# Attention heads as a software pipeline, with more PSUM banks and operands padded to 128 rows

## Chip, cores and metric

One core of a Trainium2 chip. The metric is the device time of one execution in microseconds (us). The kernel before takes 913.33 us (median of 15 runs, 910.32 to 918.20).

## The reference

Local attention with a window of 32 and 8 global tokens, for 8 batches of 8 heads (576 tokens, 64 columns), then a mixer block: token mixing (576 x 576) and a channel MLP (512 to 2048 to 512).

```python
mask = np.abs(pos[:, None] - pos[None, :]) <= 32
mask = mask | is_global[:, None] | is_global[None, :]
scores = np.where(mask, scale * np.matmul(q, k.transpose(0, 1, 3, 2)), -1e9)
attn = softmax(scores)                               # cut: written out in the reference
x = np.matmul(attn, v)                               # then heads side by side: (8, 576, 512)
a1 = alpha1 * x + beta1
u = x + lam * np.einsum('ts,bsd->btd', w_tok, a1)    # token mixing
a2 = alpha2 * u + beta2
out = u + lam * (np.maximum(a2 @ w_ch1, 0.0) @ w_ch2)
```

## The kernel before

One head (cut). Q and K are transposed through one PSUM tile (PSUM is the memory that this kernel's matmuls write their results to; a bank is a part of it). The scores are nine blocks of 128x128 (K=64, so 64 rows of the array) and five narrow matmuls for the global columns. In the value product each of the five query tiles starts with the global keys, a matmul over 8 rows, followed by one or two over 128 rows.

```python
for h in range(H):
    emit_B1(b - 1, h)                  # one piece of the batch before: load X, 1/denominator, XL, token mixing
    ...                                # loads of q, k, v, casts
    for c in range(NT):
        nc.tensor.transpose(out=trps[:, c, :], in_=qn16[:, c, :], identity=identb)
    nc.vector.tensor_copy(out=QT, in_=trps)             # QT, KT: [64, ...]
    for c in range(NT):
        nc.tensor.transpose(out=trps[:, c, :], in_=kn16[:, c, :], identity=identb)   # same bank
    nc.vector.tensor_copy(out=KT, in_=trps)
    ...                                # V's global rows, in the score tile; vg_ext: [8, 65]
    for c in CHUNKS: ...               # scores, K=64 rows
    nc.tensor.matmul(out=pvps[0:8, 512:1024], lhsT=kgT[...], rhs=QTf[:, 0:512], ...) # global scores
    nc.scalar.activation(out=PT, in_=scps[:, 0:SCORE_F], func=AF.Exp, scale=0.125)
    nc.vector.tensor_tensor(out=PT, in0=PT, in1=mask, op=ALU.mult)
    nc.scalar.activation(out=pgc, in_=pvps[0:8, PV_GCB:1024], func=AF.Exp, scale=0.125)  # [8, 640]
    for t in range(NT):
        nc.tensor.matmul(out=pvps[:, ...], lhsT=pgc[:, gsl], rhs=vg_ext, start=True, stop=False)   # 8 rows
        for ci, bi in enumerate(tbis):
            nc.tensor.matmul(out=pvps[:, ...], lhsT=PT[:, ...], rhs=rhs, start=False, ...)         # 128 rows
    ...                                # global rows into the score tile, copies to xstg and xg
# after 8 heads: store xstg to DRAM, scatter-add the global rows; emit_B1 loads it again as X
```

The softmax here doesn't subtract the row's maximum and nothing guards it: scores larger than these inputs give would overflow.

## Time and profile before

| stage | us | what fills it |
|---|---|---|
| setup | 0 to 62 | loads and preparation of weights |
| attention and token mixing | 62 to 640 | TensorE about seven tenths busy, granted clock mostly half |
| channel MLP | 640 to 912 | TensorE full, full clock |

The profile's page cuts the span in 40 slices: a digit is the busy share in tenths, and the row PEclk gives TensorE's granted clock. A timeline line gives start, duration, engine, line of the kernel, operation, output<-inputs, the weights' rows*columns, then the moving operand's rows x columns, and in brackets the idle time before it with what ended it. The prediction shows the lines of before that its reading rests on.

### The profile page before, as it was taken

The page shows a single profiled execution, that of the slowest core. Times are in us where ns is not written, and L with a number is a line of the kernel's source. Part 1 is how long each engine was busy: PE and PEld are TensorE (multiplying, and loading weights), DVE is VectorE, ACT ScalarE, POOL GpSimd, SP SyncE. Part 2 cuts the span into 40 slices and gives each one's busy share as a digit, 9 for nine tenths or more (in the row PEclk, how much of TensorE's full clock was granted, in tenths as well). Part 3 has the DMA queues.
Part 4 walks back from the last instruction along what each step waited for, and adds up shares of the span by engine and source line. Part 5 has one row for each costly group of instructions (what it writes and reads, how often), then busy time and mean ns, then how long its engine had stood idle before and what let it go on. Part 6 is the DMA issues. An engine that isn't in the chain of part 4 may idle for free.

```text
span 912.1 us, 13226 instructions
## 1 busy us (share of the span) xinstructions
PE 720.2 (79%) x5044; PEld 435.1 (48%) x5091; DVE 346.6 (38%) x865; ACT 331.9 (36%) x641; POOL 155.2 (17%) x295
## 2 busy tenths in 40 slices
PE   0158776976976976976976976935999999999998
PEld 0125544544544544544544544513665665665664
DVE  2654335635545635645645645515001001001001
ACT  0014443333333433433443333311552552552551
POOL 0035232232233232233222222100000000000000
PEclk9999999955755855755855755857999999999999
DMA  4825344454454454454454453225222222223101
GB/s 133 346 75 148 89 139 127 142 155 128 134 163 128 136 162 128 140 157 127 138 157 127 142 152 106 96 72 235 111 87 97 88 87 99 88 87 99 60 29 52
DMA packets 119111, 113.24 MB, mean 124 GB/s; under 512 B 90760, under 2 KB 91288, under 8 KB 116488
## 3 DMA queue, kind: packets, MB, share of 16 engines
q1 hardware_dynamic: 110840, 93.01, 32.2%
q0 software_dynamic: 8208, 19.40, 6.8%
q8 instruction: 40, 0.66, 0.3%
q14 instruction: 23, 0.19, 0.1%
HBM read 76.95 MB, written 35.42 MB: 123 GB/s over the span
## 4 chain that ended last, share of the span: by engine, by line
PE 72%; DVE 16%; DMA 6%; ACT 3%; issue 3%; SPq 0%; POOL 0%; POOLq 0%; ACTq 0%; DVEq 0%
PE chps L482 15%; PE hps L473 13%; PE scps L389 8%; PE tkps L293 7%; PE pvps L417 6%; PE pvps L412 4%; PE trps L374 4%; PE trps L371 4%; PE pvps L402 3%; DMA w2raw<-in_moe_w_ch_dram 3%; PE utps L307 3%; DVE XL L283 2%; DVE X L279 2%; DVE QT L372 2%; DVE KT L375 2%
## 5 line engine op out<-in xcount | busy, mean ns | idle before, releaser
L476 ACT ACTIVATE HT<-hps,bias1T 128x288 bf16<-128x288 f32 x256 | 127.7, 501 | 162.2 <-PE hps L473 135.2
L473 PE MATMUL hps<-UT,W 128*128 128x288 bf16 x1024 | 153.0, 285 | 23.2 <-DMA UT<-utdram 20.6
L482 PE MATMUL chps<-W,HT 128*128 128x512 bf16 (+1 forms) x608 | 150.4, 379 | 0.4
L473 PEld LDWEIGHTS <-W 128*128 128x128 bf16 x1024 | 98.5, 97 | 68.7 <-issue 28.9
L486 DVE TENSOR_TENSOR ob<-chps,U 128x512 f32<-128x512 f32 (+1 forms) x40 | 27.6, 690 | 242.7 <-PE chps L482 242.7
L293 PE MATMUL tkps<-XL,wtT 128*128 128x512 bf16 (+3 forms) x185 | 71.1, 492 | 32.4 <-DVE XL L283 29.4
L405 ACT ACTIVATE PT<-scps 128x1192 f16<-128x1192 f32 x64 | 74.5, 1164 | 55.8 <-PE scps L394 53.0
L359 ACT CAST vext<-vn 128x320 f16<-128x320 f32 x64 | 29.3, 458 | 178.4 <-PE scps L426 176.9
L482 PEld LDWEIGHTS <-HT 128*128 128x128 bf16 (+1 forms) x640 | 62.9, 100 | 64.1 <-issue 3.4
L389 PE MATMUL scps<-QT,KT 64*128 64x128 bf16 x576 | 72.2, 270 | 12.7 <-DVE vg_ext L384 12.1
L408 ACT ACTIVATE pgc<-pvps 8x640 f16<-8x640 f32 x64 | 44.4, 693 | 79.5 <-PE pvps L402 79.1
L412 PE MATMUL pvps<-vg_ext,pgc 8*128 8x65 f16 x320 | 71.3, 223 | 0.0
L417 PE MATMUL pvps<-voext,PT 128*128 128x65 f16 x448 | 67.9, 230 | 0.0
L360 POOL MEMSET vext<- 128x5 f16 x64 | 8.0, 125 | 334.8 <-PE scps L426 334.7
L317 POOL DMA_DIRECT2D vn<-in_v_dram x63 | 58.1, 922 | 29.2 <-ACT xg L438 25.0
L435 DVE COPY xstg<-pvps 128x320 f32<-128x320 f32 x64 | 31.3, 490 | 83.1 <-PE pvps L417 83.1
L417 PEld LDWEIGHTS <-PT 128*128 128x128 f16 x576 | 40.1, 108 | 42.8 <-DVE PT L406 22.8
L371 PE MATMUL trps<-identb,qn 128*64 128x128 bf16 x320 | 42.3, 284 | 22.4 <-DVE KT L375 22.4
L394 PE MATMUL scps<-qgT,KT 64*128 64x8 bf16 x320 | 58.5, 201 | 0.0
L372 DVE COPY QT<-trps 64x640 bf16<-64x640 bf16 x64 | 30.9, 482 | 67.1 <-PE scps L394 60.6
L374 PE MATMUL trps<-identb,kn 128*64 128x128 bf16 x320 | 41.5, 286 | 17.2 <-DVE QT L372 16.8
L389 PEld LDWEIGHTS <-KT 64*128 64x128 bf16 x576 | 51.1, 120 | 7.4 <-issue 5.9
(95 smaller groups left out, 839.8 us busy)
## 6 DMA issues: line engine op xcount, KB each, us to landing
xdram<-xstg SPq DMA_DIRECT2D x8, 1300.0 KB, 5.8
X<-xdram SPq DMA_DIRECT2D x8, 1300.0 KB, 6.8
udram<-U SPq DMA_DIRECT2D x8, 1280.0 KB, 5.7
U<-udram SPq DMA_DIRECT2D x8, 1280.0 KB, 5.8
qn<-in_q_dram SPq DMA_DIRECT2D x63, 160.0 KB, 2.9
kn<-in_k_dram SPq DMA_DIRECT2D x63, 160.0 KB, 2.4
vn<-in_v_dram POOLq DMA_DIRECT2D x63, 160.0 KB, 3.4
vo<-in_v_dram POOLq DMA_DIRECT2D x64, 128.0 KB, 3.4
```

What stands on the lines that cost most here:

```text
L293: nc.tensor.matmul(out=tkps[0:tsz, :], lhsT=wtT[0:ssz, sc, t * P : t * P + tsz], rhs=st["XL"][0:ssz, sc, :], start=(sc == 0), stop=(sc == 4),)
L317: eng.dma_start(out=dst, in_=src_flat[bh * S : bh * S + SPAD, :].rearrange("(c p) d -> p c d", p=P))
L371: nc.tensor.transpose(out=trps[:, c, :], in_=qn16[:, c, :], identity=identb)
L374: nc.tensor.transpose(out=trps[:, c, :], in_=kn16[:, c, :], identity=identb)
L389: nc.tensor.matmul(out=scps[:, bi * P : (bi + 1) * P], lhsT=KTf[:, c : c + P], rhs=QT[:, t, :], start=True, stop=True)
L394: nc.tensor.matmul(out=scps[:, GR_OFF + 8 * si : GR_OFF + 8 * si + 8], lhsT=KTf[:, c : c + P], rhs=qgT[:, 8 * h : 8 * h + 8], start=True, ...
L405: nc.scalar.activation(out=PT, in_=scps[:, 0:SCORE_F], func=AF.Exp, bias=0.0, scale=0.125)
L412: nc.tensor.matmul(out=pvps[:, t * PV_T : t * PV_T + PV_T], lhsT=pgc[:, gsl], rhs=vg_ext, start=True, stop=False)
L417: nc.tensor.matmul(out=pvps[:, t * PV_T : t * PV_T + PV_T], lhsT=PT[:, bi * P : (bi + 1) * P], rhs=rhs, start=False, stop=(ci == len(tbis) ...
L473: nc.tensor.matmul(out=hps, lhsT=W1[:, cc, ec * P : (ec + 1) * P], rhs=UT[:, cc, tsl], start=(cc == 0), stop=(cc == 3))
L476: nc.scalar.activation(out=HT[:, ec, tsl], in_=hps, func=AF.Relu, bias=bias1T[:, ec : ec + 1], scale=1.0)
L482: nc.tensor.matmul(out=chps[0:tsz, :], lhsT=HT[:, ec, t * P : t * P + tsz], rhs=W2[:, ec, :], start=(ec == 0), stop=(ec == 15))
```

## The change

Its intent: keep TensorE from waiting for the copies that empty its PSUM tiles, by separate banks and by putting another head's matmuls where it waited; spread the token mixing; and pad the operands of 8 and 64 rows with zeros to 128. The core of the diff, with cuts:

```diff
+        pads = {"pgz": [], "vgz": []}                       # two of each, zeroed once on GpSimd
+            pads["pgz"].append(pPad.tile([P, SPAD], FP16, name=f"pgz{i}"))
+            pads["vgz"].append(pPad.tile([P, PV_T], FP16, name=f"vgz{i}"))
+        for nm, shp in (("QTz", [P, NT, P]), ("KTz", [P, NT, P]), ("qgTz", [P, 64]), ("kgTz", [P, 64])):
 ...
+        def partA(b, h):   # loads, Q transposes (trq), K transposes (free part of scps), scores, exp
-                nc.vector.tensor_copy(out=QT, in_=trps)
+            nc.vector.tensor_copy(out=QT[0:64], in_=trq)      # QT is a padded tile
 ...
+        def partC(st):     # global scores, V's global rows, in a new bank smp
-                pgc = pA.tile([8, SPAD], FP16, name="pgc")
+            pgc = pads["pgz"][(b * 8 + h) % 2]
 ...
+        def partB(st, xstg, xg):   # mask, value product, global rows, copies
 ...
             for h in range(H):
+                st = partA(b, h)
+                if prev is not None:
+                    partB(prev, prev["xstg"], prev["xg"])     # value product of the head before
+                partC(st)
+                emit_B1(b - 1, h)
-                utps = psB_tr.tile([P, 4, P], FP32, name="utps")
+                utps = psB_tok.tile([P, 4, P], FP32, name="utps", tag="tkps")
```

## The prediction

> **What bounds the kernel now.** I read the page first: the slices, then the chain that ended last, then the timeline of one head, then the table by stretches of time.
>
> ```profile
> PE   0158776976976976976976976935999999999998
> PEclk9999999955755855755855755857999999999999
> PE 72%; DVE 16%; DMA 6%; ACT 3%; issue 3%; SPq 0%; POOL 0%; POOLq 0%; ACTq 0%; DVEq 0%
> ```
>
> There are three stages: setup to about 62 us, attention with token mixing from there to about 604 us (seven tenths busy on TensorE, granted clock mostly half), and the channel MLP from 640 us (saturated, full clock). The diff does not touch the first and third, about 62 and 272 us. The second, 542 us for 64 heads, is where anything can be won. The chain is mostly TensorE with a strong VectorE share, so one must see whether TensorE is full or waits. One head on the timeline:
>
> ```profile
> 403.52 0.26 PE L389 MATMUL scps<-QT,KT 64*128 64x128 bf16 x1 [0.30 <-DVE vg_ext L384]
> 405.32 0.69 PE L374 MATMUL trps<-identb,kn 128*64 128x128 bf16 x5 [0.40 <-DVE QT L372]
> 406.58 0.69 PE L371 MATMUL trps<-identb,qn 128*64 128x128 bf16 x5 [0.57 <-DVE KT L375]
> 409.72 0.27 PE L401 MATMUL pvps<-QT,kgT 64*8 64x128 bf16 x1 [0.29 <-DVE xstg L437]
> ...
> 406.45 0.76 DVE L406 TENSOR_TENSOR PT<-PT,mask 128x1192 f16<-128x1192 f16 x1
> 413.84 0.76 DVE L406 TENSOR_TENSOR PT<-PT,mask 128x1192 f16<-128x1192 f16 x1
> ```
>
> The mask multiplication comes once a head, so the period is 413.84 - 406.45 = 7.39 us. In it TensorE stands still four times, 0.30 + 0.40 + 0.57 + 0.29 = 1.56 us, each time for a VectorE copy that empties a single PSUM buffer: the transposes of Q and K share one bank (trps), pvps has one buffer, and the transpose of V's global rows sits in the score tile. So 5.83 us of TensorE are left. Once a batch something larger comes:
>
> ```profile
> PE tkps L293 <- DVE XL L283: 25.2, 6, 4.2
> 359.71 0.58 PE L293 MATMUL tkps<-XL,wtT 128*128 128x512 bf16 x1 [4.20 <-DVE XL L283]
> ```
>
> Token-mixing matmuls stand in TensorE's order ahead of heads that could run, and TensorE waits 4.2 us for two VectorE operations of 2.8 us. The batch period, from the starts of that VectorE operation (147.8 and 559.0, six batches apart), is 68.5 us.
>
> ```profile
> 364.00:366.00 2.00, 2.00 (x13) 0.91 (x11) 0.48 (x1) 1.16 (x1) 0.00 (x0) 0.50 0.00 0
> 370.00:372.00 2.00, 2.00 (x21) 1.29 (x21) 0.79 (x4) 0.82 (x3) 0.28 (x3) 1.00 0.00 0
> 314.00:316.00 2.00, 1.18 (x15) 0.81 (x14) 1.75 (x4) 0.94 (x2) 0.00 (x0) 1.00 1.02 416
> 316.00:318.00 2.00, 1.59 (x17) 0.91 (x17) 0.62 (x3) 0.64 (x3) 0.21 (x2) 0.99 0.96 376
> 318.00:320.00 2.00, 1.70 (x17) 1.26 (x16) 0.83 (x5) 0.92 (x2) 1.61 (x2) 0.50 1.15 291
> ```
>
> The columns after the stretch are its length, busy time of TensorE, weight loads, VectorE, ScalarE and GpSimd, and then the granted clock. The clock becomes full about 10 us after the dense token-mixing work begins (0.50 at 364, 1.00 at 370) and falls back once TensorE is only about 70% busy (314 to 318). That happens in every batch: some 14 to 17 us at full clock, the rest at half. The full clock shown before 165 us is only a lack of records, as the instructions there last as long as at half clock later.
>
> **What the Trainium skill says.** (1) "TensorE: Matmul & The Clock Gate", Part 1: the clock is half or full, set by how busy the array has been in a window of about 3.4 us, and falls back after an idle window. The trace agrees on the two values; it differs in that 70% busy was already too little to keep the clock. (2) The same page, Part 2, on weight loads: the time follows the columns, not the rows. Agrees: loads of 8*128 take 96 ns, of 128*128 107 ns, and the matmuls behind them 223 and 230 ns. So padding 8 or 64 rows to 128 with zeros costs TensorE nothing. (3) The same page's table of specifications: the vector engines work strictly in order. Agrees: the 4.2 us wait is an XL operation with smaller copies behind it. (4) "Trainium Kernel Development and Optimization", Best Practices: consistent bubbles can mean that PSUM ran out. The four bubbles per head are of that kind.
>
> **The change, part by part.**
> (a) Separate banks: Q's transposes keep trq, K's go into unused columns of the score tile, V's global rows and the global rows' output go to a new bank (smp). Paid for by letting the token-mixing output and the U transposes share one bank.
> (b) The loop is a software pipeline: scores of the next head are emitted before the value product of the last. In the order of the built program, a steady head reads: Q transposes, K transposes, global scores, small V transpose, scores, value product, global rows, with scores and value product at times exchanged. Nearly each wait of before now has another block of matmuls ahead of it.
> (c) Token-mixing matmuls are spread over heads 3 to 7 and later, in groups of five between heads, instead of one block.
> (d) Zero padding to 128 rows: 12 GpSimd memsets before the first gathers; per head nothing.
>
> TensorE's work per head, from first start to next block's start. At half clock (403 to 412 us): scores 1.14, value product 1.72, global rows 0.43, transposes 0.69 twice, global scores 0.62, V transpose 0.26, sum 5.55 us. At full clock (309 to 318 us): 0.71, 1.34, 0.25, 0.44 twice, 0.46, 0.19, sum 3.83 us.
> Per batch at full clock: 8 x 3.83 = 30.6, token mixing 5 x 1.12 = 5.6 and U transposes about 2.5 (both from the tail, 627 to 638 us), gathers' transposes 0.9: 39.6 us.
> VectorE per head, means of its rows: 0.325 + 0.482 + 0.480 + 0.765 + 0.489 + 0.155 + 0.145 + 0.211 + 0.059 = 3.11 us; per batch 24.9, plus U 3.4, UT 3.2, X and XL 5.6, small ones 1.9: 39.0 us. ScalarE: 1.164 + 0.693 + 0.457 + 0.458 + 0.402 + 0.197 = 3.37 us a head, 27 a batch.
> So two engines have 39 us each. They don't meet perfectly: VectorE still works in order, and X with XL hold it for 5.6 us, during which K's copy is late. I choose 1 us of friction per head and 3 us per batch for X and XL: 51 us. TensorE will go cold in that hole and need some 10 us to warm again; 10 us at half clock do the work of 10 x 3.83/5.55 = 6.9 us, so 3 us more: 54 us a batch against 68.5. Seven batches with token mixing: 7 x 14.5 = 101 us.
> The first batch has none to warm TensorE: 7.39 to about 6.0 us a head, 8 x 1.4 = 11 us. The memsets hold the first gathers up by perhaps 4 us (a guess from 0.48 us for a VectorE memset of 64x512). The tail from 604 to 638 us (store, scatter, load, X, XL) stays, and so does the MLP.
> Sum: 912 - 101 - 11 + 4 = 804, say 805 us.
>
> **The rivals.**
> R1, the clock stays half. The token mixing is now less dense, and if it no longer opens the clock, a batch costs 8 x 5.55 + 25 x 0.43 + 4.5 + 0.9 = 60.5, with friction 63 us: 7 x 5.5 + 7 = 45 us gained, 867 us. For it: heads at half clock never opened it, with TensorE 79% busy. Against: groups of five token-mixing matmuls still follow scores with no gap, and TensorE should be over 90% busy. I give it one in six.
> R2, the clock stays full nearly throughout, padding perhaps helping since more rows then work: 45 to 47 us a batch, about 750 us. For it: the MLP stage never lost the clock. Against: the X and XL hole, and VectorE's 39 us plus semaphores. One in eight.
> R3, a transfer takes the place of the removed waits. The chain store, scatter, load takes 14.7 us in the quiet tail (604.3 to 619.0) and about 20 us amid traffic (195.3 to 214.8); VectorE's in-order queue has X some four heads after the store, 17 to 20 us at the new pace. A wait of up to 4 us a batch is possible, 28 us in all. Loads of Q and K land in 2.4 to 2.9 us with two buffers, and DMA is 0.48 busy, so 0.6 at the new pace: no new bound.
> R4, the shared bank (tkps with U transposes) chains token mixing to VectorE. Against: other matmuls stand between the groups.
>
> **Range and chances.** The middle case gives 805; R3 lifts it to 833, R1 to 867, R2 lowers it to 750. I take 760 to 860. All but an unforeseen wait lie well below 894 us: faster 0.95, same 0.04, slower 0.01.
>
> **What would show it.** Right: the batch period near 54 us; the four waits per head of TensorE (on QT, KT, vg_ext, xstg copies) nearly gone; means per instruction unchanged apart from the clock; MLP stage still 272 us; VectorE over 70% busy in attention. The clock: full for over half of each batch. Wrong: clock at half throughout (R1), or TensorE or VectorE waiting on X's load (R3), or scores waiting for K's copy at a microsecond each head because VectorE has become the bound.

## The result, and the profile after

The changed kernel takes **736.75 us** (median of 9 runs, 732.89 to 737.66), the ratio to before is 0.8055 (95% interval 0.8036 to 0.8075). The direction was right; the time is below the range of 760 to 860 us.

The page of the kernel after:

```profile
PE   0126887876949858588595826999999999999997
PEclk9999997897978969889698777999999999999999
PE 58%; DMA 20%; DVE 12%; ACT 6%; issue 3%; POOL 1%; SPq 0%; POOLq 0%; ACTq 0%; DVEq 0%
```

The clock, half in most of attention before, is full in most of it now (mean over the span 0.923, before 0.803; both means count the time ahead of a kernel's first clock record as full, before up to 165 us and after up to some 82 us, though the durations there are those of half clock). The chain that ended last has lost much of its TensorE share and gained DMA, mostly the round trip of X through DRAM. The MLP still takes 274 us (460 to 734), so all of the gain is in attention. Mask multiplications of the kernel after, one a head:

```profile
99.75 0.78 DVE L444 TENSOR_TENSOR PT<-PT,mask 128x1192 f16<-128x1192 f16 x1
103.28 0.78 DVE L444 TENSOR_TENSOR PT<-PT,mask 128x1192 f16<-128x1192 f16 x1
```

A head takes 3.5 us where nothing disturbs it, against 7.39 before. A batch takes 46.5 us: VectorE's operation on X starts at 168.76 and, five batches later, at 401.45. It was 68.5.

The waits between 120 and 440 us of the kernel after (engine, line, what it waited for: us in total, times, longest):

```profile
DVE rden L277 <- DMA X<-xdram: 25.6, 7, 5.2
PE pvps L447 <- DVE vgz L434: 21.1, 5, 5.4
PE scps L408 <- DVE KTz L399: 11.1, 18, 1.9
PE smp L432 <- DVE xg L473: 8.5, 7, 6.1
PE tkps L294 <- DVE XL L284: 4.6, 2, 3.1
```

TensorE's regular waits per head on the copies of Q, K and xstg are gone or small. A new one stands in their place, once a batch: VectorE, which takes its instructions in order, stands at the reciprocal of X until the load has landed, and TensorE behind it for the copy of V's global rows.

```profile
260.98 0.40 DVE L277 RECIPROCAL rden<-X 128x40 f32<-128x40 f32 x1 [3.83 <-DMA X<-xdram]
261.50 0.21 PE L447 MATMUL pvps<-vgz,pgz 128*128 128x65 f16 x1 [4.39 <-DVE vgz L434]
```

The table by stretches round this hole (length; busy time of TensorE, weight loads, VectorE, ScalarE, GpSimd; granted clock; DMA share; GB/s):

```profile
252.00:256.00 4.00, 3.17 (x50) 2.23 (x48) 3.09 (x12) 3.55 (x9) 3.10 (x8) 1.00 0.63 147
256.00:260.00 4.00, 1.07 (x8) 0.57 (x8) 1.15 (x3) 1.43 (x4) 1.63 (x2) 0.88 0.94 343
264.00:268.00 4.00, 2.05 (x20) 1.80 (x21) 3.97 (x5) 1.92 (x4) 1.17 (x2) 0.50 0.71 166
272.00:276.00 4.00, 4.00 (x43) 2.23 (x42) 2.80 (x8) 1.16 (x1) 1.78 (x2) 0.91 0.14 27
```

The clock falls in the hole and is back some 14 us later; from 276 to 300 us it stays full with TensorE at 3.06 to 3.98 of 4 us, in the thinnest stretch hardly denser than what lost it in the kernel before.

Now the line that the prediction passed over: the value product at full clock, first in the kernel before and then in the kernel after.

```profile
308.96 0.24 PE L417 MATMUL pvps<-vext,PT 128*128 128x65 f16 x2
309.13 0.20 PE L412 MATMUL pvps<-vg_ext,pgc 8*128 8x65 f16 x1
309.26 0.24 PE L417 MATMUL pvps<-voext,PT 128*128 128x65 f16 x2
309.43 0.20 PE L412 MATMUL pvps<-vg_ext,pgc 8*128 8x65 f16 x1
...
310.30 0.23 PE L426 MATMUL scps<-vext,PT 128*8 128x65 f16 x2
```
```profile
254.64 0.19 PE L447 MATMUL pvps<-vgz,pgz 128*128 128x65 f16 x1
254.67 0.22 PE L452 MATMUL pvps<-vext,PT 128*128 128x65 f16 x2
254.74 0.19 PE L447 MATMUL pvps<-vgz,pgz 128*128 128x65 f16 x1
254.76 0.23 PE L452 MATMUL pvps<-voext,PT 128*128 128x65 f16 x2
...
255.16 0.23 PE L461 MATMUL smp<-vext,PT 128*8 128x65 f16 x2
```

Read the **starts**, not the durations. Before, one period of an 8-row matmul and two of 128 rows takes 309.43 - 309.13 = 0.30 us; after, 254.76 - 254.67 = 0.09 us. The block took 1.34 us (308.96 to 310.30, 13 matmuls) and takes 0.52 us (254.64 to 255.16, 14 matmuls), at the same clock. The durations hardly tell it: each matmul lasts about 0.2 us in both and starts, in the kernel after, as little as 0.03 us behind the one ahead of it, so they overlap.

### The profile page after: what moved, and what is told of

Same layout as the page of the kernel before. It is cut to its first block, busy times and chain, and to the rows that moved or that the text cites. A ratio compares the mean times of both kernels' runs of the same rounds, so it can differ in the third digit from the quotient of the medians.

```text
span 734.2 us, 13252 instructions
## 1 busy us (share of the span) xinstructions
PE 568.1 (77%) x5044; PEld 354.7 (48%) x5091; DVE 336.3 (46%) x865; ACT 324.2 (44%) x641; POOL 160.6 (22%) x307
## 4 chain that ended last, share of the span: by engine, by line
PE 58%; DMA 20%; DVE 12%; ACT 6%; issue 3%; POOL 1%; SPq 0%; POOLq 0%; ACTq 0%; DVEq 0%
PE chps L539 18%; PE hps L530 16%; PE tkps L294 7%; DMA X<-xdram 6%; PE scps L408 4%; DMA xdram<-xg,gsc 4%; DMA w2raw<-in_moe_w_ch_dram 3%; ACT PT L419 3%; DVE X L280 3%; ACT HT L533 2%; DMA g_rep<-in_global_idx_dram 2%; PE utps L308 2%; PE trq L392 2%; PE scps L398 2%; DMA vo<-in_v_dram 1%
## 5 line engine op out<-in xcount | busy, mean ns | idle before, releaser
L408 PE MATMUL scps<-QTz,KTz 128*128 128x128 bf16 x576 | 55.3, 231 | 13.4 <-DVE KTz L399 13.3
L447 PE MATMUL pvps<-vgz,pgz 128*128 128x65 f16 x320 | 40.8, 199 | 24.6 <-DVE vgz L434 21.5
L438 ACT ACTIVATE pgz<-pvps 8x640 f16<-8x640 f32 x64 | 44.2, 691 | 32.5 <-PE pvps L429 32.1
L374 POOL DMA_DIRECT2D vo<-in_v_dram x64 | 54.0, 844 | 4.1 <-ACT voext L383 2.8
L444 DVE TENSOR_TENSOR PT<-PT,mask 128x1192 f16<-128x1192 f16 x64 | 49.3, 770 | 9.7 <-ACT PT L419 8.3
L408 PEld LDWEIGHTS <-KTz 128*128 128x128 bf16 x576 | 40.5, 102 | 21.3 <-DVE KTz L399 17.0
L411 PE MATMUL scps<-qgTz,KTz 128*128 128x8 bf16 x320 | 47.8, 176 | 0.0
L398 PE MATMUL scps<-identb,kn 128*64 128x128 bf16 x320 | 35.5, 238 | 11.8 <-ACT PT L419 8.0
L378 ACT CAST kn<-kn 128x320 bf16<-128x320 f32 x64 | 28.9, 454 | 24.6 <-DMA kn<-in_k_dram 16.0
L301 DVE TENSOR_TENSOR U<-tkps,X 128x512 f32<-128x512 f32 (+1 forms) x40 | 27.5, 688 | 22.3 <-PE tkps L294 22.1
```

Source lines behind the costliest of these rows:

```text
L374: nc.gpsimd.dma_start(out=vo, in_=vf[bh * S + 64 : bh * S + S, :].rearrange("(c p) d -> p c d", p=P))
L398: nc.tensor.transpose(out=scps16[0:64, KTRС + c * P : KTRС + (c + 1) * P], in_=kn16[:, c, :], identity=identb)
L408: nc.tensor.matmul(out=scps[:, bi * P : (bi + 1) * P], lhsT=KTf[:, c : c + P], rhs=QT[:, t, :], start=True, stop=True)
L411: nc.tensor.matmul(out=scps[:, GR_OFF + 8 * si : GR_OFF + 8 * si + 8], lhsT=KTf[:, c : c + P], rhs=g["qgT"][:, 8 * h : 8 * h + 8], start=True,
L438: nc.scalar.activation(out=pgc[0:8, :], in_=pvps[0:8, PV_GCB:1024], func=AF.Exp, bias=0.0, scale=0.125)
```

## The experiments

Theories for the 68 us between the prediction and the time: **A**, a change of the number of rows from one matmul to the next (between 8 and 128 above all) costs time, and padding removes it; **B**, the clock depends on how many rows work, and padding opens or keeps it; **C**, it all comes from the order and the banks, and padding is worth nothing, as I had written. Later, for what is left: **R3**, the wait for X.

### e1 and e2: the kernel before with the padding alone

Edit e1 (e2 has only pgz and vgz):

```diff
+        pads = {}   # pgz, vgz, QTz, KTz, qgTz, kgTz: two tiles each of 128 rows, zeroed once
-                QT = pA.tile([64, NT, P], BF16, name="QT")
+                QT = pads["QTz"][bh % 2]
-                vg_ext = pA.tile([8, PV_T], FP16, name="vg_ext")
+                vg_ext = pads["vgz"][bh % 2]
-                pgc = pA.tile([8, SPAD], FP16, name="pgc")
+                pgc = pads["pgz"][bh % 2]
```

> The kernel before with only the zero padding (exponentials of the global rows and their values from 8 rows to 128, Q, K and their global rows from 64 to 128). Theory A (a change between 8-row and 128-row operands costs TensorE about 0.09 us each time, ten times a head): the value product falls from 1.72 to about 0.7 us a head, it is on the chain, so 64 x 0.9 = 55 to 60 us less, about 855 us, clock still half in most of attention. Theory B (the clock monitor counts rows, padding opens the clock): clock over 0.9, below 830 us. Theory C (all comes from the pipeline and the banks): 912 us, no change.

> The kernel before with only the 8-row operands padded to 128, Q and K left at 64 rows. Theory A: as the run with all padding within 1%, about 855 us, value product 0.7 us. Theory B: less than the run with all padding, as the score matmuls keep 64 rows. Theory C: 912 us.

Measured: e1 848.10 us, ratio 0.9266 (0.9230 to 0.9301); e2 863.44 us, ratio 0.9431 (0.9393 to 0.9469). Padding alone, with every bank and the order as before, takes off 65 us; the 8-row operands alone 50 us. The value product of e1 at half clock, behind the wait that is as before:

```profile
373.04 0.69 PE L378 MATMUL trps<-identb,qn 128*64 128x128 bf16 x5 [0.57 <-DVE KTz L382]
373.73 0.29 PE L424 MATMUL pvps<-vext,PT 128*128 128x65 f16 x2
373.82 0.25 PE L419 MATMUL pvps<-vgz,pgz 128*128 128x65 f16 x1
373.88 0.30 PE L424 MATMUL pvps<-voext,PT 128*128 128x65 f16 x2
...
374.55 0.28 PE L433 MATMUL scps<-vext,PT 128*8 128x65 f16 x2
```

It takes 374.55 - 373.73 = 0.82 us, against 1.72 us (407.27 to 408.99) for the same 13 matmuls before. C falls.

### e3 and e4: the kernel after without the padding, and with that of the 8-row operands alone

```diff
-            pads["pgz"].append(pPad.tile([P, SPAD], FP16, name=f"pgz{i}"))      # e3
+            pads["pgz"].append(pPad.tile([8, SPAD], FP16, name=f"pgz{i}"))      # e3
-        for nm, shp in (("QTz", [P, NT, P]), ("KTz", [P, NT, P]), ...)          # e3 and e4
+        for nm, shp in (("QTz", [64, NT, P]), ("KTz", [64, NT, P]), ...)        # e3 and e4
```

> The changed kernel without any padding: 8-row and 64-row operands as before, pipeline and banks as changed. Theory A: the value product is back at 1.34 us a head at full clock, 64 x 0.8 = 51 us more, 785 to 800 us, clock still mostly full, as the prediction had it. Theory B: the clock falls to half in most of attention, over 840 us. Theory C: 737 us.

> The changed kernel with only the 8-row operands padded, Q and K at 64 rows. Theory A: within 1.5% of the changed kernel, 735 to 748 us (the scores may cost 0.1 us a head more). Theory B: the clock loses much of its share, over 770 us. Theory C: 737 us.

Measured: e3 between 810.21 and 840.70 us in four runs (two of them slower, the profiled one among them; the fast ones 810.21 and 818.30, ratio 0.8900, 0.8833 to 0.8967); e4 754.70 us, ratio 0.8247 (0.8216 to 0.8278), clock 0.89 to 0.90. So without padding the change is worth about 95 to 103 us, close to the 107 that I had predicted for the whole of it, and the padding another 74 to 82 us. A named 785 to 800 us for e3, 735 to 748 for e4 and at most 1% between e1 and e2; all three missed, by 7 to 18 us, so the 8-row operands are not the whole. B's numbers (e1 below 830 us, e3 over 840, e4 over 770) missed too.

Padding Q and K takes off 18 us here (e4 to after) and 15 us on the kernel before (e2 to e1). The clock has a part in the 18. The first batch, which has no token mixing, takes 38.6 us in e4 and 30.4 in after (first to ninth mask), which is 8 of the 18. In after the clock opens in that batch, seen by K's transposes:

```profile
77.65 0.74 PE L398 MATMUL scps<-identb,kn 128*64 128x128 bf16 x5
81.76 0.44 PE L398 MATMUL scps<-identb,kn 128*64 128x128 bf16 x5
```

In e4 it is still half at 103 us: the value product takes 0.88 us (103.32 to 104.20), against 0.51 in after. Over several batches the mean granted clock is 0.59 in e3 (232 to 475 us, the slow run) with TensorE busy 93% of the time, 0.73 in e4 (220 to 438) with 81%, and 0.86 in after (225 to 413) with 76%: the more rows, the more clock, though TensorE is less busy. The change of rows has a part too: the score block takes 0.71 us in e2 (405.72 to 406.43, with a change to 128 rows behind it) and 0.64 in e1 (403.76 to 404.40, without), both at full clock; 64 times 0.07 is an estimate of 4.5 us. How the rest of the 15 to 18 us divides is not separated.

### e5: as many 8-row matmuls, fewer changes

```diff
+                    last = t % 2 == 1
+                    if not last:
                         nc.tensor.matmul(out=pvps[...], lhsT=pgc[:, gsl], rhs=vg_ext, ...)   # 8 rows
                     for ci, bi in enumerate(tbis): ...                                       # 128 rows
+                    if last:
+                        nc.tensor.matmul(out=pvps[...], lhsT=pgc[:, gsl], rhs=vg_ext, ...)   # 8 rows
```

> The kernel before, with no padding; only the place of the 8-row matmuls in the value product's five groups is changed (last in the second and fourth group, first in the others), so that two of them stand next to each other twice and the changes between 8 and 128 rows fall from ten to six a head. The number of 8-row matmuls and all other instructions are the same. Theory A1 (it is the change of the row count that costs): padding those five in e2 took 50 us, 0.78 us a head, 0.078 a change; four changes fewer make 64 x 4 x 0.078 = 20 us, so about 893 us, and the value product falls from 1.72 to about 1.38 us at half clock. Theory A2 (each matmul over 8 rows is slow in itself, 0.16 us, whatever stands beside it): 913 us, product still 1.72 us.

Measured: 887.89 us, ratio 0.9728 (0.9697 to 0.9760), 25 us less. The value product of e5, half clock:

```profile
405.58 0.29 PE L419 MATMUL pvps<-vext,PT 128*128 128x65 f16 x2
405.68 0.30 PE L419 MATMUL pvps<-voext,PT 128*128 128x65 f16 x2
405.92 0.23 PE L427 MATMUL pvps<-vg_ext,pgc 8*128 8x65 f16 x1
405.96 0.24 PE L414 MATMUL pvps<-vg_ext,pgc 8*128 8x65 f16 x1
406.13 0.40 PE L419 MATMUL pvps<-voext,PT 128*128 128x65 f16 x4
...
406.85 0.27 PE L430 MATMUL scps<-vext,PT 128*8 128x65 f16 x2
```

The second 8-row matmul starts 0.04 us after the first, the 128-row one behind it 0.17 us later. The same 13 matmuls take 1.72 us with eight changes inside the block (before), 406.85 - 405.58 = 1.27 us with four (e5) and 0.82 us with none (e1): a straight line of **0.11 us a change**. At full clock it is the same: (1.34 - 0.52 x 13/14) / 8 = 0.11 us. So it is the change that costs, not the few rows: A1 holds, A2 falls. My 0.078 a change was too small: it divided what e2's run gained (50 us, 0.78 us a head) by ten changes, while the block loses eight and gets 0.90 us shorter, not all of which shows in the run's time.

### e6: banks and padding without the order across heads

```diff
-                if prev is not None:
-                    partB(prev, prev["xstg"], prev["xg"])
                 partC(st)
+                partB(st, xstg, xg)
```

> The kernel after with its banks and its padding, but the value product emitted with its own head instead of after the next head's scores. In the built order the scheduler still puts some work of the next head ahead of a value product, but the next head's K transposes (which use the score tile) now come right behind the global scores, so they wait for the exponential of this head. Theory S (the cross-head order carries a good part of the gain): 0.5 to 1 us more a head, 770 to 800 us, with TensorE waiting for the exponential's read of the score tile, and more time at half clock. Theory T (the scheduler reorders by itself, and banks and padding do it all): 737 to 750 us. Neither expects more than e1's 848.

Measured: 746.31 us, ratio 0.8179 (0.8156 to 0.8202). This is within theory T, that the scheduler reorders across heads once the banks allow it: the hand-written order is worth only about 10 us. My case S, 770 to 800, was wrong.

### e11 and e12: does the clock see the rows?

The nine wide score matmuls of each head are repeated eight times into the same place, over 64 rows (e11, on e4) or over 128 rows with zeros (e12, on after).

```diff
+            for rep in range(8):
+                for c in CHUNKS:
+                    for bi in CHUNK_BLOCKS[c]:
+                        t = BLOCKS[bi][0]
+                        nc.tensor.matmul(out=scps[:, bi * P : (bi + 1) * P], lhsT=KTf[:, c : c + P], rhs=QT[:, t, :], start=True, stop=True)
```

> The kernel of e4 (Q and K over 64 rows, all else as after) with the nine 128-column score matmuls of each head issued eight more times into the same places (the result stays right): some 72 extra matmuls of 64 rows, in long runs with no change of row count inside. It is a pair with the next run, whose same matmuls work over 128 rows. Theory B1 (the clock follows how much of the array's rows stream): 64-row runs do not open or keep the clock, so the repeats run at half clock, 72 x 0.11 = 8 us a head more: about 1200 us, mean clock under 0.8. Theory B2 (the clock follows only how densely columns stream, and padding helped it only by taking away the row-change holes): the clock stays full in the repeats, 72 x 0.055 = 4 us a head more: about 1010 us, within 20 us of the next run.

> The kernel after with the same eight repeats of the nine score matmuls, over 128 rows with zeros. Both theories expect the full clock nearly throughout and 4 us a head more: about 990 us, mean clock over 0.95.

Measured: e11 1162.99 us (2 runs), mean clock 0.803 (too high, see below); e12 978.96 us (2 runs), mean clock 0.954. From e11 runs of repeats, the token mixing ahead of one of them, and two stretches:

```profile
68.22 7.86 PE L407 MATMUL scps<-QTz,KTz 64*128 64x128 bf16 x72 [0.38 <-DVE KTz L397]
208.18 1.49 PE L294 MATMUL tkps<-XL,wtT 128*128 128x512 bf16 x3 [0.22 <-issue]
209.60 7.86 PE L407 MATMUL scps<-QTz,KTz 64*128 64x128 bf16 x72
223.64 4.19 PE L407 MATMUL scps<-QTz,KTz 64*128 64x128 bf16 x72
```
```profile
244.00:248.00 4.00, 3.36 (x50) 2.53 (x48) 1.06 (x5) 1.67 (x4) 0.93 (x3) 0.85 0.07 12
284.00:288.00 4.00, 4.00 (x40) 4.00 (x39) 0.00 (x0) 0.00 (x0) 0.97 (x2) 0.50 1.07 239
```

and the same places of e12:

```profile
69.25 5.39 PE L409 MATMUL scps<-QTz,KTz 128*128 128x128 bf16 x66
242.12 1.49 PE L294 MATMUL tkps<-XL,wtT 128*128 128x512 bf16 x3 [0.22 <-issue]
243.40 5.70 PE L409 MATMUL scps<-QTz,KTz 128*128 128x128 bf16 x72
```

A run of 72 takes 7.86 us at half clock and 4.19 at full. In e12 the clock opens within the first run, which starts at 68.25 us (six repeats, then the 66 shown) with no token mixing ahead of it, and again within the run at 243.40, which comes out of a hole. In e11 the same run at 68.22 stays at half, and so do those that follow, up to the one at 209.60, though it comes behind the same token-mixing matmuls as e12's at 243.40. (The clock column shows 1.00 for e11 from the start up to 244 us; up to 217 those are missing records, as in the kernel before up to 165 us, so go by the durations.) In e11 the clock opens between 217 and 223.64 us, while single token-mixing matmuls over 128 rows run, and in the next two batches at the same place (runs of 4.19 us from 323.73 and 425.54). It lasts some 24 us, with token mixing between the runs of repeats, and is lost in the stretch from 244, after a run of repeats and with 3.36 of 4 us busy; then it stays half through 44 us of unbroken work, most of it over 64 rows (248 to 292, TensorE 4.00 of 4.00 in each stretch).

So dense work over 64 rows did not open the clock; over 128 rows, zeros included, it did. B1 is right about opening, and its 1200 us is near; B2's 1010 us falls. Whether 64 rows alone would keep a clock that is open, e11 doesn't show, as 128-row work came in between, and what lost it (the gaps or the rows) isn't separated.

### e9 and e10: the token mixing two heads later

```diff
-                emit_B1(b - 1, h)
+                late = b * 8 + h - 8 - 2
+                if late >= 0:
+                    emit_B1(late // 8, late % 8)
```

e10 also cuts the two large VectorE operations on X into five.

> The kernel after, each piece of the token mixing emitted two heads later, so that the load of X, which waited for the scatter, has 7 us more. Theory R3 (VectorE stands in its queue at X until the load lands, about 3.7 us a batch, and TensorE behind it about 4.4 us plus the time at half clock that follows): the wait of VectorE for X goes, 3 to 5 us a batch, 7 batches: 21 to 35 us; but after the last batch two more pieces lie bare, up to 5 us back. So 705 to 725 us. Rival (the hole is the two VectorE operations of 5.2 us themselves, and the clock falls anyhow): 730 to 740 us, with the wait for X gone and TensorE's wait for the copy of V's rows still some 3 us a batch.

> As the run before, and the two large VectorE operations on X in five pieces each, so that copies for the heads can go between. Theory R3 plus in-order queue: both waits gone, clock full for nearly the whole of attention, 700 to 715 us. Rival (the scheduler keeps the ten pieces together, or VectorE's extra instructions cost what the hole did): within 5 us of the run before.

Measured: e9 733.76 us, ratio 0.8045 (0.8017 to 0.8073); e10 728.94 us, ratio 0.7975 (0.7958 to 0.7993), within the rival's 5 us of e9, with VectorE's wait for X not gone but 34.7 us in the whole run. The edit did not do what it was meant to. In e9:

```profile
DVE rden L277 <- DMA X<-xdram: 25.8, 7, 5.5
```

The wait is the same, because the built order of VectorE's instructions still has the reciprocal behind the mask of the batch's fifth or even fourth head: the scheduler, not the place in the source, decides. These runs say nothing on R3.

### e13 and e14: the work on X held back by a dependency

```diff
             elif piece == 1:
                 st["rden"] = pB1.tile([P, NT, 8], FP32, name="rden")
+                nc.vector.tensor_copy(out=st["rden"][0:1, 0, 0:1], in_=dep[0:1, 0:1])   # dep: masked PT, head 6
                 nc.vector.reciprocal(out=st["rden"], in_=st["X"][:, :, DM:XW])
 ...
+                late = b * 8 + h - 8 - 5     # pieces 1 to 7; the load stays at h == 0
```

e14 is e13 with the operations on X in five pieces each.

> The kernel after, with the work on X held back for certain: one copy of a single element from the masked scores of the sixth head into the tile of the reciprocals must come first, so VectorE's order has the reciprocal one head later (in the built order it is behind the mask of the sixth head, in after and in e9 behind the fifth's or fourth's). The load of X stays where it was. Theory R3: VectorE's wait for X, 25.6 us in seven batches, goes nearly wholly, and so does TensorE's wait behind it on V's copy, 21 us; 15 to 30 us less, 705 to 722 us. Rival (the clock falls anyhow while VectorE has the 5.6 us of X and XL, and TensorE waits there all the same): 728 to 736 us.

> As e13, and the two operations on X and XL in five pieces each, with the heads' copies between them (the built order shows them between the pieces). R3 with the in-order queue: 3 to 10 us less than e13, 700 to 715 us. Rival: the pieces change nothing, within 3 us of e13.

Measured: e13 **702.99 us** (5 runs, 702.19 to 708.33), ratio to before 0.7687 (0.7666 to 0.7708); e14 728.27 us, ratio 0.7982 (0.7940 to 0.8024). VectorE in e13:

```profile
257.35 0.13 DVE L278 CAST rden<-PT 1x1 f32<-1x1 f16 x1
258.83 0.40 DVE L279 RECIPROCAL rden<-X 128x40 f32<-128x40 f32 x1
259.79 2.80 DVE L281 TENSOR_TENSOR X<-X,rden 128x2560 f32<-128x2560 f32 x1
263.45 0.76 DVE L445 TENSOR_TENSOR PT<-PT,mask 128x1192 f16<-128x1192 f16 x1
264.15 2.81 DVE L285 TENSOR_TENSOR XL<-X,LA 128x2560 bf16<-128x2560 f32 x1
```

No bracket stands behind the reciprocal: X has landed before VectorE comes to it. VectorE's wait for X, 25.6 us in the kernel after, is down to 1.2 us (once), and TensorE's wait for the copy of V's rows fell from 21.1 to 10.3 us:

```profile
PE pvps L448 <- DVE vgz L435: 10.3, 6, 2.3
```

A later batch takes some 42 us (masks of the same head) instead of 46.5, which for seven batches is about 31 of the 34 us that e13 is below the kernel after. R3 holds, as far as one edit can say that both holds back the work on X and moves the token mixing behind it five heads later. The clock still falls once a batch, since the two operations of 2.8 us still hold VectorE up. Cutting them in five (e14) makes it worse by 25 us instead of better; its batch takes about 44.5 us, and the stretch from the last mask to the MLP is about 9 us longer. Which of the scheduler's moves does that is left open. e13 beats both kernels.

## Why the prediction was wrong

**The step that failed** is part (d), "per head nothing", and the conclusion ahead of it that padding "costs TensorE nothing". That it costs nothing is right, but it gains: the padded value product was put into the table of TensorE's work at 1.34 us at full clock and 1.72 at half, as measured over 8 rows, and takes 0.52 and 0.82. I compared durations of single matmuls (223 and 230 ns), which overlap; the distance of the starts, which is what a block costs, showed the change of rows plainly in the kernel before.

**The term.** Read from the starts in the kernel after (252 to 256 us), a head's TensorE work at full clock differs from the prediction's list by the value product (0.52, not 1.34) and the scores (0.64, not 0.71): 2.94 us, not 3.83. Eight heads make 7.1 us, and the batch is 7.5 us shorter than predicted: 46.5, not 54. Seven batches: 52 of the 68 us. That the rest of the batch's sum (friction, X and XL, warming) was sized rightly does not follow; its parts were not measured one by one.

**The clock of the first batch.** I let the first eight heads run at half clock for want of token mixing to warm TensorE, 11 us gained. From the first to the ninth mask they took 131.81 - 70.38 = 61.4 us before and 103.28 - 72.87 = 30.4 us after, 31 us gained, 20 more. The value product of a head in that batch takes 0.51 us (101.91 to 102.42), so the clock was full there with no token mixing about; e4, with Q and K over 64 rows, has it half there, and e11 and e12 show that the rows have to do with it. The two terms make 72 us, and what was left over the other way (the tail and rounding) 4.

**The clock of the other batches** came as predicted, full for over half of each, but not for the reason given, that TensorE would be over 90% busy. In e3, without padding, TensorE was 93% busy and the clock 0.59 on average (a slow run); the padding raised it. So that e3's gain of 95 to 103 us is near the 107 I had predicted is in part luck. Nor is my "70% busy was already too little" a rule: rows were not looked at there.

**The rivals.** R1 did not come. R2 named the right time, about 750 us, and even padding, but for one in eight and only as to the clock. R3, outside the central sum, came as described: VectorE waits 25.6 us for X in seven batches, 3.7 each, inside "up to 4 us a batch", and e13 shows the cost with what follows it. That less friction than my 1 us a head made it good is an inference from the total.

**What held.** The four waits per head go (order and banks alone, e3, about 95 to 103 us). The MLP stays, 274 against 272 us. VectorE is busy 71% of the time from 120 to 440 us (predicted over 70%). The memsets hold up the first gathers by 63.78 - 59.06 = 4.7 us, predicted 4, shown by GpSimd's timeline, after and before:

```profile
59.30 0.63 POOL L329 MEMSET pgz<- 128x640 f16 x1 [57.98 <-PE wps L231]
...
63.78 1.10 POOL L345 DMA_INDIRECT qg_g<-in_q_dram,hg_idx  x1 [0.18 <-issue]
```
```profile
59.06 1.10 POOL L328 DMA_INDIRECT qg_g<-in_q_dram,hg_idx  x1 [57.74 <-PE wps L231]
```

## What to carry to other kernels

Cost a block of small matmuls by the distance between its starts, at equal clock, and compare neighbours of different shape: a jump there is a cost that mean durations hide, and padding or regrouping may remove it. Where a scheduler sets the order, check the built order before drawing anything from an edit of the source; a tiny true dependency moves an instruction for certain. A wait of an in-order engine for a transfer can be worth more than its length: 25.6 us of VectorE's waiting for X went to 1.2, and 34 us of the time (e13).

## What the Trainium skill lacked or had wrong

- "TensorE: Matmul & The Clock Gate", Part 2, on weight loads, and the row on small K in "Why this matters for your kernels" (a single K=32 matmul takes as long as one with K=128): right for equal neighbours, but neither says that going from 8 to 128 rows or back costs time. "TensorEngine Tiling (Array Packing)", Key Properties, comes nearest: a change of tiling mode drains TensorE. It gives no figure and doesn't say whether plain matmuls over fewer rows are such a change, and no run here shows that they are. Here 0.11 us a change, at half and full clock (blocks of 1.72, 1.27 and 0.82 us with eight, four and no changes); 50 us of 913 in e2.
- The same page, Part 1, has the clock full after a busy window of some 3.4 us. In e11 runs of nothing but 64-row matmuls, 7.86 us each, left it at half from 68 to 217 us, while work over 128 rows, zeros included, opened it within a run of 5.39 or 5.70 us (e12). No page found says that rows count.
- The same part's table names an idle window for the fall; its section on PSUM-queue cycling says that short idle times between groups can do it too, without a figure. In e11 the clock fell in a stretch with TensorE 3.36 of 4 us busy, in the kernel before at about 70%; the kernel after kept it at 3.06 of 4.
- "Perfetto Trace Analysis", Optimizing Scalar/DVE Operations, says that breaking up instructions may help if VectorE isn't saturated but causes bubbles. Here, with VectorE busy about 3.2 of 4 us in attention (e13), it cost 25 us (e13 703, e14 728) and, in the order of e9, gained 5 (e9 734, e10 729); the page's "may" is to be taken seriously.
